# Reordering the value tiles, the weight folds and the first query logits in a fused linear-attention and dense kernel

## Chip, core and metric

The kernel runs on one core of a Trainium2 chip. The metric is the device time of one execution in microseconds (us), lower is better. Each kernel was executed several times, and the runs of the kernel before and of the kernel compared with it were taken on the same chip in the same rounds. A ratio is the mean time of one kernel's runs over the mean of the other's in the same rounds, so it isn't quite the ratio of the medians quoted beside it.

## The reference, cut to what matters

```python
# x: 2048 x 512, 32 heads of 16
qkv = x @ wqkv
pq, pk = q @ w_phi, k @ w_phi                     # per head
phi_q = concat(softmax(pq), softmax(-pq))         # the same for k
kv, z = phi_k^T v, sum(phi_k)
a = (phi_q kv) / (phi_q z + 1e-6) @ wo
b = relu(x @ w1) @ w2                             # 512 -> 1376 -> 512
g = sigmoid(sum(x * gate_w))
out = g * a + (1 - g) * b
```

## The kernel before

TensorE does nearly everything. At its start it computes the hidden layer of the first 512 rows. Then it multiplies `w_phi` into the query and key weights (eight **weight folds**, four for the query, four for the key). Then, for each of 16 tiles of 128 rows, it computes query and key **logits** (a query half and a key half of four matmuls each), the **value tile** (four matmuls), the product of key features and values (`kv`), and some **units** of the hidden layer of later rows (four matmuls each). The **gate remainder** is 16 short matmuls for 512 rows: the last 96 columns of the hidden layer, which fill no unit, and the column of the gate. The folds need the transposed weights, which arrive by DMA in two transfers, query first.

A matmul group writes to one of eight PSUM banks. VectorE (DVE) or ScalarE (ACT) copies the result out, and the next group that takes the bank waits for that copy. The helper `p.op` records an operation with the events that it waits for (`after`) and the event that it sets (`ev`). `free[bank]` is the event that frees a bank.

```python
def pre(i):                                   # a weight fold
    which, dt = i // 4, i % 4
    bank = (0, 1, 6, 7)[i % 4]
    after = [f"wqk{which}"] + [...] + free[bank]
    ...                                       # 4 matmuls into the bank
    # even i: copied by VectorE, odd i: by ScalarE
    free[bank] = [f"pc{i}"]

def atile(m):                                 # logits: query in bank 0, key in bank 1
    ...                                       # 8 matmuls, then exp(+x), exp(-x) on ScalarE
    free[1], free[0] = [emk], [f"em{m}"]

def vtile(m, eng="act", bank=2):              # a value tile, copied by `eng`
    ...

gatecol(0)
vtile(0, "dve")
vtile(1, "act", nextbank())                   # nextbank(): 3, 4, 5 in rotation
for i in range(4):
    pre(i)
vtile(2, "dve")
for i in range(4, 8):
    pre(i)
rest(0)                                       # gate remainder
...
for m in range(NT):
    atile(m)
    if m >= LAG: kv(m - LAG)
    if m + 3 < NT: vtile(m + 3)
    for u in mid[m]: unit(*u)                 # two units in the first turn
```

The softmax here doesn't subtract the row's maximum and nothing guards it: scores larger than these inputs give would overflow.

## Time and profile before

| what | value |
|---|---|
| median of the first 3 timed runs | 146.91 us (146.79 to 146.95) |
| the profiled execution itself | 147.59 us, span 146.3 us |
| TensorE busy | 98% of the span |
| folds 0 to 3 start / folds 4 to 7 start | 15.30 / 17.57 us |
| tile 1's logits start | 23.33 us |

The profile is of one execution, and that execution took 0.64 us longer than the longest of the three timed ones. The lines of this profile are in the prediction.

### The profile page before, as it was taken

Reading aid. Unit: us, or ns where it says so; the run is one execution under the profiler, and the core shown is the slowest. Engines: PE = TensorE matmul, PEld = TensorE weight load, DVE = VectorE, ACT = ScalarE, POOL = GpSimd, SP = SyncE. Lnnn points to the kernel's source line nnn. Section 1 sums busy time; section 2 is a strip of 40 time slices with the busy share of each in tenths; the row PEclk is TensorE's granted clock in tenths of the full one; section 3 lists DMA queues with packets and bytes.
Section 4 is the critical chain, followed back from the end, with each engine's and each line's share of the span. In section 5 each row is a group of like instructions: output and inputs, shape, how many; then the busy total and the mean of one; then the engine's idle time right before and its main releaser. Section 6 shows DMA issues by size and latency. Waiting matters only on the chain.

```text
span 146.3 us, 2520 instructions
## 1 busy us (share of the span) xinstructions
PE 143.0 (98%) x970; PEld 72.3 (49%) x970; DVE 91.7 (63%) x156; ACT 72.4 (49%) x124; POOL 52.2 (36%) x62
## 2 busy tenths in 40 slices
PE   8999799999999999999999999999999999999994
PEld 3444564444455545544645555554444444444443
DVE  4338627777687878678698977674445555555342
ACT  4134467798778778887878862022221111111150
POOL 2013002778768678688869820300000000000000
DMA  5998998033549984335333431354333223222213
GB/s 150 262 276 163 231 167 186 3 69 72 76 80 328 179 201 73 72 72 108 78 72 75 104 72 31 81 108 117 85 82 78 72 72 76 72 72 74 72 44 106
DMA packets 46517, 16.12 MB, mean 110 GB/s; under 512 B 40392, under 2 KB 46120, under 8 KB 46504
## 3 DMA queue, kind: packets, MB, share of 16 engines
q1 hardware_dynamic: 46352, 15.92, 50.3%
q8 instruction: 8, 0.13, 0.4%
q10 hardware_dynamic: 152, 0.03, 0.1%
q14 instruction: 5, 0.04, 0.1%
HBM read 4.15 MB, written 2.10 MB: 43 GB/s over the span
## 4 chain that ended last, share of the span: by engine, by line
PE 86%; SPq 7%; DMA 4%; DVE 1%; issue 0%
PE PS L483 26%; PE PS L328 18%; PE PS L272 18%; PE PS L492 9%; PE PS L404 8%; SPq L185 4%; DMA PHQ<-in_A_wqkv_dram 4%; PE PS L458 3%; PE PS L426 3%; PE PS L284 2%; SPq L162 2%; SPq L175 1%; PE PS L306 1%; DVE WQK L506 1%; SPq L182 0%
## 5 line engine op out<-in xcount | busy, mean ns | idle before, releaser
L483 PE MATMUL PS<-W,HT 128*128 128x512 bf16 (+4 forms) x187 | 40.6, 366 | 0.0
L372 POOL TENSOR_TENSOR EB<-EB,SC 128x1024 bf16<-128x1024 bf16 x15 | 28.9, 1930 | 23.4 <-DVE SC L370 23.4
L348 ACT ACTIVATE EB<-PS 128x480 bf16<-128x480 f32 (+1 forms) x44 | 30.1, 756 | 14.2 <-PE PS L328 14.2
L497 ACT ACTIVATE TFA<-PS,GT 128x512 bf16<-128x512 f32 x16 | 11.0, 687 | 42.7 <-PE PS L492 36.6
L272 PE MATMUL PS<-XT,W 128*128 128x512 bf16 x128 | 30.7, 379 | 0.0
L328 PE MATMUL PS<-WQK,XT 128*128 128x480 bf16 x128 | 28.5, 366 | 0.0
L368 DVE TENSOR_REDUCE ZB<-EB 128x64 f32<-128x1024 bf16 x15 | 18.3, 1220 | 14.7 <-ACT EB L348 14.7
L506 DVE SCALAR_TENSOR_TENSOR WQK<-PS,OMG,TFA 128x512 bf16<-128x512 f32 (+2 forms) x17 | 12.2, 719 | 23.6 <-ACT TFA L497 22.4
L483 PEld LDWEIGHTS PS<-W,HT 128*128 128x128 bf16 (+1 forms) x187 | 17.0, 98 | 17.4
L258 ACT ACTIVATE HT<-PS 128x512 bf16<-128x512 f32 x35 | 20.3, 614 | 7.4 <-PE PS L520 5.6
L328 PEld LDWEIGHTS PS<-WQK,XT 128*128 128x128 bf16 x128 | 12.5, 98 | 13.6
L383 DVE TENSOR_REDUCE ZB<-EB 128x64 f32<-128x1024 bf16 x16 | 18.6, 1164 | 0.0
L272 PEld LDWEIGHTS PS<-XT,W 128*128 128x128 bf16 x128 | 12.0, 98 | 13.2
L392 POOL TENSOR_TENSOR EB<-EB,SC 128x512 bf16<-128x512 bf16 x16 | 16.9, 1059 | 1.3
L404 PE MATMUL PS<-WV,XT 128*128 128x512 bf16 x64 | 16.2, 378 | 0.0
L492 PE MATMUL PS<-WO,OT 128*128 128x512 bf16 x64 | 16.1, 378 | 0.0
L468 DVE TENSOR_TENSOR WQK<-PS,RDEN 128x512 bf16<-128x512 f32 x16 | 11.1, 692 | 0.5
L492 PEld LDWEIGHTS PS<-WO,OT 128*128 128x128 bf16 x64 | 6.1, 97 | 7.2
L414 ACT ACTIVATE VS<-PS 128x512 bf16<-128x512 f32 x14 | 8.5, 608 | 2.0 <-PE PS L404 2.0
L370 DVE RECIPROCAL SC<-ZB 128x64 f32<-128x64 f32 x16 | 8.8, 553 | 0.5
L458 PEld LDWEIGHTS PS<-KVNZ,PHQ 128*128 128x128 bf16 x128 | 6.1, 97 | 3.6
L404 PEld LDWEIGHTS PS<-WV,XT 128*128 128x128 bf16 x64 | 5.4, 97 | 4.8
(57 smaller groups left out, 85.7 us busy)
## 6 DMA issues: line engine op xcount, KB each, us to landing
out_dram<-WQK SPq DMA_DIRECT2D x15, 128.0 KB, 1.7
W<-in_B_w_dram SPq DMA_DIRECT2D x2, 640.0 KB, 5.8
W<-in_B_w_dram SPq DMA_DIRECT2D x3, 256.0 KB, 3.8
WV<-in_A_wqkv_dram SPq DMA_DIRECT2D x1, 512.0 KB, 6.5
WO<-in_A_wo_dram SPq DMA_DIRECT2D x2, 256.0 KB, 3.0
W<-in_B_w_dram SPq DMA_DIRECT2D x1, 352.0 KB, 5.1
OT<-in_A_x_dram SPq DMA_DIRECT2D x2, 128.0 KB, 2.3
W<-in_B_w_dram SPq DMA_DIRECT2D x2, 128.0 KB, 3.0
```

Of the source, the lines that this page charges most:

```text
L258: p.op("act", lambda e: e.activation(dst, src, ACT.Relu), after=[f"h{c}_{kt}"], ev=ev)
L272: p.op("pe", lambda e, t=t: e.matmul(PS[:, bank, :], W1[:, t, kt * P:(kt + 1) * P], XT[:, t, c * 512:(c + 1) * 512], start=(t == 0), stop= ...
L328: p.op("pe", lambda e, dt=dt, which=which: e.matmul(PS[:, which, 0:DE], XT[:, dt, m * P:(m + 1) * P], WQK[:, which, dt * DE:(dt + 1) * DE] ...
L348: p.op("act", lambda e: e.activation(dst, s_, ACT.Exp, scale=scale), after=[f"qk{m}"] + busy, ev=ev)
L368: p.op("dve", lambda e: e.tensor_reduce(zk, ek, AX.X, ALU.add), after=[emk, f"cst{b}"], ev=f"zk{m}")
L372: p.op("pool" if m < NT - 1 else "dve", lambda e: e.tensor_tensor(EB[:, b, 3, :].rearrange("p (g f) -> p g f", f=DH), EB[:, b, 2, :].rearr ...
L383: p.op("dve", lambda e: e.tensor_reduce(ZB[:, b, 0:64].rearrange("p (h s) -> p h s", s=2), bass.AP(tensor=EB, offset=base, ap=[[EBS, P], [ ...
L392: p.op("pool", lambda e: e.tensor_tensor(EB[:, b, 0, :].rearrange("p (h s f) -> p h s f", h=H, s=2)[:, :, 1, :], EB[:, b, 1, :].rearrange( ...
L404: p.op("pe", lambda e, dt=dt: e.matmul(PS[:, bank, :], XT[:, dt, m * P:(m + 1) * P], WV[:, dt, :], start=(dt == 0), stop=(dt == NDT - 1)), ...
L483: p.op("pe", lambda e, kt=kt, M=M: e.matmul(PS[:, bank, 0:n], HT[0:M, kt, m * P:(m + 1) * P], W2[0:M, kt, cs], start=(kt == 0), stop=(kt = ...
L492: p.op("pe", lambda e, t=t: e.matmul(PS[:, bank, :], OT[:, t, m * P:(m + 1) * P], WO[:, t, :], start=(t == 0), stop=(t == NDT - 1)), after ...
L506: p.op("dve", lambda e: e.scalar_tensor_tensor(out=OSB[:, ob, cs], in0=PS[:, bank, 0:n], scalar=OMG[:, m:m + 1], in1=TFA[:, m % 2, cs], op ...
```

## The change

The intent is to give TensorE work while it waits for the two weights. Value tile 2 goes ahead of the folds. Value tile 3 and the query half of tile 0's logits go between the two groups of folds. For that the folds take other banks, and the gate remainder is the last thing ahead of tile 0's key half.

```diff
         def pre(i):
-            bank = (0, 1, 6, 7)[i % 4]
+            bank = (0, 1, 6, 7, 1, 7, 2, 6)[i]
...
-        def atile(m):
+        def atile(m, part=None):
...
-            if m == 0:
-                order = [(dt, w) for w in (0, 1) for dt in range(NDT)]
+            if part is not None:
+                order = [(dt, part) for dt in range(NDT)]
...
+            if part == 0:
+                return
...
         vtile(1, "act", nextbank())
+        vtile(2, "dve")
         for i in range(4):
             pre(i)
-        vtile(2, "dve")
+        vtile(3, "act", 6)
+        atile(0, 0)
         for i in range(4, 8):
             pre(i)
         rest(0)
...
-            atile(m)
+            atile(m, None if m else 1)
...
-            if m + 3 < NT:
+            if 0 < m < NT - 3:
                 vtile(m + 3)
```

More of the change, by code (lines that the diff above doesn't have):

```diff
@@ L332, in atile @@
                     + ([f"pc{4 * which + c}" for c in range(4)] if m == 0 and dt == 0 else []),
-                    ev=(f"qk{m}" if i == 7 else None))
+                    ev=(f"qk{m}" if part != 0 and i == len(order) - 1 else None))
+            if part == 0:
+                return
             src = PS[:, 0:2, 0:DE].rearrange("p a (h f) -> p a h f", h=H)
```

## The prediction

> **What bounds the kernel now.** I read the page first, then the chain that ended last in order of time, then the waits of TensorE, then the timeline of the 12 us in which the change works. Page and chain:
>
> ```profile
> PE 143.0 (98%) x970; PEld 72.3 (49%) x970; DVE 91.7 (63%) x156; ACT 72.4 (49%) x124; POOL 52.2 (36%) x62
> ...
> PE 86%; SPq 7%; DMA 4%; DVE 1%; issue 0%
> ...
> 12.41 5.12 DMA PHQ<-in_A_wqkv_dram
> 17.53 0.04 issue
> 17.57 1.01 PE PS L306 x16
> 18.59 0.69 PE PS L284 x16
> 19.28 1.62 PE PS L328 x8
> 20.90 0.86 PE PS L404 x4
> 21.76 1.73 PE PS L272 x8
> ```
>
> TensorE is busy 98% of the span and is 86% of the chain. Before 17.57 us the chain is a DMA, the second transposed projection weight; from 17.57 us to 143.73 us it is TensorE alone. So whatever moves TensorE's stream near 20 us moves the end by as much, and nothing later absorbs it. How much there is to win, the waits of TensorE say:
>
> ```profile
> PE PS L306 <- DMA PHQ<-in_A_wqkv_dram: 0.9, 2, 0.5
> PE PS L231 <- DVE ONE L207: 0.4, 1, 0.4
> ```
>
> Only two waits lie in the stretch of the change: the two halves of the weight folds (L306), each waiting for its weight. The timeline of that stretch:
>
> ```profile
> 13.95 0.69 DVE L412 CAST VS<-PS 128x512 bf16<-128x512 f32 x1
> ...
> 15.30 1.01 PE L306 MATMUL PS<-Wbd,PHQ 128*128 128x120 bf16 x16 [0.52 <-DMA PHQ<-in_A_wqkv_dram]
> 15.72 1.22 DVE L311 CAST WQK<-PS 128x480 bf16<-128x480 f32 x2 [1.07 <-PE PS L306]
> 15.93 1.03 ACT L313 ACTIVATE WQK<-PS 128x480 bf16<-128x480 f32 x2 [0.52 <-PE PS L306]
> ...
> 16.15 1.03 PE L404 MATMUL PS<-WV,XT 128*128 128x512 bf16 x4
> ...
> 17.57 1.01 PE L306 MATMUL PS<-Wbd,PHQ 128*128 128x120 bf16 x16 [0.40 <-DMA PHQ<-in_A_wqkv_dram]
> ...
> 19.12 1.78 PE L328 MATMUL PS<-WQK,XT 128*128 128x480 bf16 x8
> ...
> 20.94 1.83 ACT L348 ACTIVATE EB<-PS 128x960 bf16<-128x960 f32 x2 [1.06 <-PE PS L328]
> ...
> 23.33 1.78 PE L328 MATMUL PS<-WQK,XT 128*128 128x480 bf16 x8
> ```
>
> The shown ends of matmuls overlap their successors, so I count by starts. Value tiles 0 and 1 start at 12.89 and are issued by 12.89 + 2 x 0.86 = 14.61; the first fold starts at 15.30: a gap of 0.69. Value tile 2 starts at 16.15 and is issued by 17.01; the fifth fold starts at 17.57: a gap of 0.56. In all **1.25 us** (0.92 in the view, which lets the drain of the pipe count as busy). That is 0.85% of 146.91 us and the most that this change can save.
>
> **What the Trainium skill says.** (1) "TensorE: Matmul & The Clock Gate", section "Wait — 56ns, not 53.3ns?": warm back-to-back matmuls start N / 2.4 GHz + 2.5 ns apart, 215.7 ns at N = 512. The trace agrees: the chain counts four of them at 0.86 us. (2) Same page, section "What's actually happening": the clock falls back after an idle window of some 3.4 us. The gaps here stay well below, and the trace has a granted clock of 1.00 through them, so I charge no slow matmuls. (3) "PSUM — Partial Sum Buffer", section "PSUM bank collisions raise a hardware error": the hardware doesn't arbitrate two engines on one bank, so a semaphore must guard it. Hence a matmul group that takes a bank again stands behind the copy that empties it. No wait of this kind stops TensorE in the trace before. (4) Same page, section "Engine vs sequencer instructions": the queues of VectorE and ScalarE are strict FIFO. The trace agrees in that the copies of a pair come one after the other (0.652 us each, 1.22 us for two, so 0.57 from start to start). So a value copy put ahead of fold copies delays them.
>
> **The change part by part.** No operation is added or removed; order and banks change. All parts keep their durations. The new order on TensorE is value tiles 0, 1, 2; folds 0 to 3; value tile 3 into bank 6; the query half of tile 0's logits; folds 4 to 7; the gate remainder; the key half; then the loop, which no longer has value tile 3. Terms from the trace: a value tile 0.86; a half of the logits 1.62 / 2 = 0.81; a fold (15.30 to 16.15, four) 0.21; the remainder (18.42 to 19.12) 0.70. From a fold's first matmul to its copy 0.42 (15.30 to 15.72); from the start of a value tile's last matmul (13.54) to its copy 0.41. VectorE to TensorE release 0.06 (the constant's memset ends at 0.32, the first matmul starts at 0.38), used for ScalarE also, an estimate.
>
> Step 1, value tile 2 before the folds. It takes bank 2 from value tile 0, whose copy ends at 13.95 + 0.69 = 14.64. So it starts at 14.70 in place of 14.61 (gap **0.09**) and is issued by 15.56. The first weight had landed by 15.29, so the first wait is gone: folds 0 to 3 take 15.56 to 16.41.
>
> Step 2, value tile 3 in bank 6. Bank 6 holds fold 2, and fold 2 is copied by VectorE, third in a queue: first the copy of value tile 2 (ready at 14.70 + 0.65 + 0.41 = 15.76, to 16.45), then fold 0 (starts 0.61 after, the spacing of a 0.69 us operation in this trace, at 16.37), then fold 2 (0.57 later, 16.94, ends 17.60). Value tile 3 can start at 17.66, though TensorE was free at 16.41: a gap of **1.25**. This is the new wait that matters. The tile is issued by 18.52, the query half by 19.33 (its folded weights are ready).
>
> Step 3, folds 4 to 7, 19.33 to 20.18. The second weight landed by 17.57, hidden. Their banks 1, 7, 2, 6 are free (value tile 3's copy on ScalarE, 18.73 to 19.33, is done before fold 7 at 19.97). The remainder takes until 20.88. The key half needs all four copies: VectorE's second runs 20.32 to 20.97, ScalarE's second 20.42 to 20.99, so it starts at 21.05: a gap of **0.17**. Issued by 21.86.
>
> Step 4, the first tile of the loop. Before, value tile 3 and two hidden-layer units (0.86 + 1.73 = 2.59 us) lay between tile 0's logits and tile 1's, and covered the exponentials. Now only 1.73 us lie there. The exponentials start 0.40 after the last logit matmul's start (20.54 to 20.94), here 21.66 + 0.40 = 22.06, take 1.83 and end at 23.89. Tile 1, whose banks they empty, starts at 23.95; TensorE was free at 23.59: a gap of **0.36**. From then on each turn has its value tile again and more than the 2.1 us cover, and the trace shows no wait.
>
> Sum: old gaps 1.25 go, new gaps 0.09 + 1.25 + 0.17 + 0.36 = 1.87 come. Tile 1's logits start at 23.95 in place of 23.33, with the same work done: **+0.62 us**. Nothing behind absorbs it, as TensorE waits nowhere later; 146.91 + 0.62 = 147.5.
>
> **Rivals.** (a) The intent holds, the value tile and the query half fill both waits and no new one comes: -1.25, 145.7 us. For it: the order of the operations is just long enough to cover the landing of the weights at 15.3 and 17.6. Against it: bank 6, whose copy is third in VectorE's queue. (b) Only the bank-6 wait is real and the exponentials don't hold tile 1: gaps 1.51, +0.26, 147.2 us. For it: step 4 rests on an overlap of 0.36 us only. Against it: 1.83 of exponentials, 0.40 of drain and 0.06 of release are all from rows, and 2.29 minus a matmul's 0.20 exceeds 1.73. (c) The transfers are hidden, but each of four restarts of TensorE costs 0.1 us more than the one release that I could measure: +1.0, 147.9 us. For it: the release is read off one wait at the kernel's start. (d) VectorE becomes a bound for a while, because all its copies come late: against it, VectorE is 63% busy, and the first use of tile 0's key features by TensorE is at 33.5 us, when POOL has had them since 26.6.
>
> **Range and chances.** (b) and (c) lie 0.3 to 0.4 us on either side of 147.5, and runs of the kernel before spread over 0.16 us. I take 146.9 to 148.1 for eight times in ten; what is outside is mostly (a) in full or in part. Two per cent is 2.94 us: faster would need more than twice the idle time that exists, slower nearly five times my net. So within 2% at 0.98, and 0.01 for each side.
>
> **What would show it.** In the waits of TensorE the two DMA waits are gone, and in their place stand a wait of L404 for VectorE's fold copy (near 1.1 to 1.3 us, near 17.7 us in time), a small one of L328 for a fold copy near 21.0, and one of L328 for ScalarE's exponentials near 23.9. VectorE's timeline has the value copy, then two fold copies in a row, ending near 17.6. The two starts to compare: tile 1's logits, 23.33 before. If they come earlier than 23.33, steps 2 and 4 are wrong; if the wait at value tile 3 is there and the one at tile 1 isn't, (b) holds. A fold start later than 15.6, or a granted clock below 1.0 after the long gap, would be outside of all that I reckoned with.

## The result

The changed kernel took 148.66 us (median of 6 runs, 148.27 to 149.25) against 146.94 us of the kernel before (6 runs, 146.79 to 147.27), a ratio of 1.0116 with a 95% interval of 1.0089 to 1.0143. It is slower by 1.7 us where 0.6 us was predicted, and lies above the predicted range.

The page of the changed kernel's profile (its profiled run took 148.50 us, near the median) has these lines for engine shares and for the chain that ended last, which answer to the first two shown of before:

```profile
PE 142.6 (97%) x954; PEld 72.5 (49%) x970; DVE 91.7 (62%) x156; ACT 72.5 (49%) x124; POOL 52.1 (35%) x62
...
PE 95%; DVE 2%; ACT 1%; issue 1%; DVEq 0%
```

The DMA has gone from the chain. In its place VectorE and ScalarE stand in it. The chain in order of time (start, length, engine and line), in the stretch of the change:

```profile
13.21 2.72 PE PS L406 x12
15.94 0.02 issue
15.96 0.69 DVE VS L414
16.65 1.14 DVE WQK L311 x2
17.79 0.05 issue
17.84 1.04 PE PS L406 x4
...
21.22 0.10 issue
21.32 0.98 PE PS L328 x4
22.30 0.02 issue
22.32 1.84 ACT EB L350 x2
24.17 0.05 issue
24.21 0.98 PE PS L328 x4
```

Value tiles 0 to 2 run through; then the chain passes through VectorE, which copies value tile 2 and then two folds, and comes back to TensorE at 17.84 us with value tile 3. It leaves TensorE again at 22.32 us for ScalarE's exponentials and comes back with tile 1's logits at 24.21 us. The waits of TensorE say the same (who waited for whom, total, times, longest):

```profile
PE PS L406 <- DVE WQK L311: 1.1, 1, 1.1
PE PS L231 <- DVE ONE L207: 0.4, 1, 0.4
PE PS L328 <- ACT EB L350: 0.2, 1, 0.2
```

Both waits for the weights are gone, and two waits of the predicted kind are there. The two smaller ones that were predicted are in the list of the weight loader (PEld), which loads a matmul's weights ahead of it:

```profile
PEld PS L406 <- DVE VS L414: 0.4, 1, 0.4
PEld PS L328 <- DVE WQK L311: 0.2, 1, 0.2
```

The view shows TensorE's waits somewhat short, because a matmul's modelled end lies after the time at which the next one could have started (a 128x512 matmul is shown 378 ns long on average, and four follow each other in 0.86 us). From the starts in the timeline of the changed kernel

```profile
13.07 2.85 PE L406 MATMUL PS<-WV,XT 128*128 128x512 bf16 x12
...
15.76 1.00 PE L306 MATMUL PS<-Wbd,PHQ 128*128 128x120 bf16 x16
...
19.52 1.00 PE L306 MATMUL PS<-Wbd,PHQ 128*128 128x120 bf16 x16
20.36 0.86 PE L284 MATMUL PS<-W,XT 128*128 128x97 bf16 x16
```

the gaps are: 13.07 + 3 x 0.862 = 15.66 to 15.76, so 0.10 within the value tiles (value tile 2 starts at 14.89, 1.82 after value tile 0, where two tiles take 1.72); 15.76 + 0.85 = 16.61 to 17.84, so 1.23 ahead of value tile 3; 20.36 + 0.69 = 21.05 to 21.32, so 0.27 ahead of the key half; and 21.32 + 0.81 + 1.73 = 23.86 to 24.21, so 0.35 ahead of tile 1. In all 1.95 us.

So the stretch can be measured by one number: the time from the start of value tile 0 to the start of tile 1's logits. It holds the same work in all orders: four value tiles 3.45, folds 0.85 + 0.84, remainder 0.69, tile 0's logits 1.62, two units 1.73, together 9.18 us. What exceeds 9.18 is gaps. (Spans are printed to 0.1 us, so what is counted to the end is good to 0.05 us.) In the changed kernel it is 24.21 - 13.07 = 11.14 us. In the first profile of the kernel before it was 23.33 - 12.89 = 10.44 us. That explains 0.70 us of the difference, not 1.7. From tile 1's logits to the end both profiles have the same: 147.2 - 24.21 = 122.99 and 146.3 - 23.33 = 122.97 us. The missing microsecond isn't behind the change. It had to be in the profile that the change was compared with.

### The profile page after: what moved, and what is told of

The parts are those of the page before. It is cut to its first block, busy times and chain, and to the rows that moved or that the text cites. A ratio compares the mean times of both kernels' runs of the same rounds, so it can differ in the third digit from the quotient of the medians.

```text
span 147.2 us, 2503 instructions
## 1 busy us (share of the span) xinstructions
PE 142.6 (97%) x954; PEld 72.5 (49%) x970; DVE 91.7 (62%) x156; ACT 72.5 (49%) x124; POOL 52.1 (35%) x62
## 4 chain that ended last, share of the span: by engine, by line
PE 95%; DVE 2%; ACT 1%; issue 1%; DVEq 0%
PE PS L485 25%; PE PS L328 18%; PE PS L272 17%; PE PS L406 9%; PE PS L494 9%; PE PS L522 5%; PE PS L460 3%; PE PS L428 3%; PE PS L284 2%; PE PS L231 2%; ACT EB L350 1%; DVE WQK L311 1%; DVE WQK L508 1%; PE PS L237 1%; PE PS L306 1%
## 5 line engine op out<-in xcount | busy, mean ns | idle before, releaser
L485 PE MATMUL PS<-W,HT 128*128 128x512 bf16 (+4 forms) x183 | 40.1, 366 | 0.2
L272 PE MATMUL PS<-XT,W 128*128 128x512 bf16 x122 | 29.9, 379 | 0.3
L406 PE MATMUL PS<-WV,XT 128*128 128x512 bf16 x60 | 15.3, 379 | 1.3 <-DVE WQK L311 1.1
```

The source lines that it names most:

```text
L272: p.op("pe", lambda e, t=t: e.matmul(PS[:, bank, :], W1[:, t, kt * P:(kt + 1) * P], XT[:, t, c * 512:(c + 1) * 512], start=(t == 0), stop= ...
L406: p.op("pe", lambda e, dt=dt: e.matmul(PS[:, bank, :], XT[:, dt, m * P:(m + 1) * P], WV[:, dt, :], start=(dt == 0), stop=(dt == NDT - 1)), ...
L485: p.op("pe", lambda e, kt=kt, M=M: e.matmul(PS[:, bank, 0:n], HT[0:M, kt, m * P:(m + 1) * P], W2[0:M, kt, cs], start=(kt == 0), stop=(kt = ...
```

## The experiments

Theory A: the predicted waits are right, but the profile of the kernel before is of an execution in which the second weight landed late, so that the gaps that the change removes are in most runs much smaller than 1.25 us. Rival B: the profile is typical, and the changed kernel loses a further microsecond that its own profile doesn't show. Fourteen runs were made, two of them of the unchanged kernels, with 5 rounds each and 6 executions of the kernel (4 in pad_after, 5 in late_w_after). All gave correct results. They ran in four batches on different chips, so a ratio is always to the kernel before in the same batch. Starts and stretches are those of one profiled execution each.

| run | median us | ratio to before (95% interval) | value tile 0 starts | tile 1's logits start | between | to the end |
|---|---|---|---|---|---|---|
| before, first profile | 146.94 | 1 | 12.89 | 23.33 | 10.44 | 122.97 |
| r_before | 146.68 | 0.9988 (0.9970 to 1.0005) | 12.89 | 22.33 | 9.44 | 122.97 |
| pad_before | 147.05 | 1.0006 (0.9980 to 1.0032) | 13.05 | 22.22 | 9.17 | 122.98 |
| late_w_before | 147.18 | 1.0026 (1.0008 to 1.0044) | 13.50 | 22.67 | 9.17 | 123.03 |
| later_w_before | 148.28 | 1.0087 (1.0069 to 1.0105) | 13.78 | 24.08 | 10.30 | 123.02 |
| after, first profile | 148.66 | 1.0116 (1.0089 to 1.0143) | 13.07 | 24.21 | 11.14 | 122.99 |
| r_after | 148.61 | 1.0115 (1.0093 to 1.0138) | 13.68 | 24.82 | 11.14 | 122.98 |
| pad_after | 148.88 | 1.0133 (1.0115 to 1.0151) | 13.08 | 24.22 | 11.14 | 122.98 |
| late_w_after | 148.38 | 1.0109 (1.0089 to 1.0129) | 12.98 | 24.11 | 11.13 | 122.99 |
| later_w_after | 148.67 | 1.0117 (1.0097 to 1.0137) | 13.26 | 24.39 | 11.13 | 123.01 |
| free_bank | 148.49 | 1.0100 (1.0070 to 1.0131) | 13.56 | 23.84 | 10.28 | 123.66 |
| late_copy | 148.06 | 1.0084 (1.0046 to 1.0121) | 13.01 | 22.99 | 9.98 | 123.71 |
| all_three | 148.25 | 1.0074 (1.0041 to 1.0107) | 13.37 | 23.86 | 10.49 | 123.14 |
| between | 147.51 | 1.0026 (0.9995 to 1.0057) | 13.25 | 22.67 | 9.42 | 123.63 |
| late_copy5 | 147.22 | 1.0031 (1.0007 to 1.0054) | 13.43 | 23.41 | 9.98 | 122.99 |
| between5 | 146.55 | 0.9985 (0.9964 to 1.0005) | 13.46 | 22.82 | 9.36 | 122.98 |

### Both kernels profiled again

The kernel before, unchanged:

> The kernel before, unchanged, profiled a second time. The first profiled run took 147.59 us against a median of 146.94, so its profile may show a late arrival of the second folded weight. Theory A (my gaps of 1.25 us were those of an unusually slow run): the new profile has a span near 145.6 to 145.9 us and the fifth fold starts at 16.8 to 17.2 us in place of 17.57, so that the two gaps ahead of the folds come to about 0.6 to 0.9 us. Rival B (the profile was typical and the profiled execution is just longer): the fifth fold again at 17.5 to 17.6 us, span 146.3. Ratio 1.00 either way.

The timeline of this second profile of the kernel before, TensorE's rows:

```profile
12.89 1.89 PE L404 MATMUL PS<-WV,XT 128*128 128x512 bf16 x8
14.61 1.00 PE L306 MATMUL PS<-Wbd,PHQ 128*128 128x120 bf16 x16
15.45 1.03 PE L404 MATMUL PS<-WV,XT 128*128 128x512 bf16 x4
16.58 1.01 PE L306 MATMUL PS<-Wbd,PHQ 128*128 128x120 bf16 x16
...
22.33 1.78 PE L328 MATMUL PS<-WQK,XT 128*128 128x480 bf16 x8
```

Value tile 0 starts at the same 12.89 us. But the first fold follows the value tiles at once (14.61), and the fifth starts at 16.58 us in place of 17.57: the gaps are 0 and 16.58 - (15.45 + 0.86) = 0.27 us, not 0.69 and 0.56. Tile 1's logits start 1.00 us earlier than in the first profile, and the span is 145.3 us in place of 146.3. TensorE's list of waits has no DMA any more. Only the weight loader, whose idle time isn't covered by modelled ends, still shows one:

```profile
PEld PS L306 <- DMA PHQ<-in_A_wqkv_dram: 0.6, 1, 0.6
```

The profiled execution took 146.62 us this time. The first took 147.59, which is above all eleven runs of the kernel before in these rounds (146.68 to 147.31). Theory A holds in kind: the first profile was of a slow execution. Its numbers were missed on the far side (gaps of 0.6 to 0.9 us, a fifth fold at 16.8 to 17.2 and a span from 145.6 us were expected), and this second execution is a fast one, below all eleven of the kernel before. With its stretch the kernels should differ by 11.14 - 9.44 = 1.70 us; 0.0115 of 147 us is 1.69. That a single fast profile fits so well is in part luck: the gap also depends on when value tile 0 starts, and what it is in the median execution wasn't measured.

Where the late weight comes from can be followed one step back. SyncE (SPq) issues the two weight transfers, here in the first and then in the second profile:

```profile
6.60 8.06 SPq L185 DMA_TRANSPOSE PHQ<-in_A_wqkv_dram  x2
6.59 7.31 SPq L185 DMA_TRANSPOSE PHQ<-in_A_wqkv_dram  x2
```

In the chain of the first profile the second weight's transfer starts at 12.41 us and lands at 17.53; in that of the second it is

```profile
11.54 4.99 DMA PHQ<-in_A_wqkv_dram
```

so it lands at 16.53. Of the 1.00 us, 0.87 was lost before the transfer began. In the twelve profiles in which nothing was put between the two transfers, their issue takes 8.06 us in the first profile and 6.92 to 7.67 in the other eleven: the first profile is the odd one out. Why its issue took longer isn't known.

The changed kernel, unchanged:

> The changed kernel, unchanged, profiled a second time. Ratio 1.010 to 1.013 again. The chain of the first profile starts on TensorE at 0.38 us and never passes through a weight's arrival, so theory A expects the span to differ from 147.2 us by just as much as the start of value tile 0 differs from 13.07 us (within 0.1 us), and the distance from there to tile 1's logits to be 11.14 us again. Rival: the distance itself varies by several tenths.

Value tile 0 started 0.61 us later (13.68 for 13.07), tile 1's logits 0.61 later (24.82), and the span is 147.8 for 147.2 us. The 11.14 us between are the same to the hundredth; the other profiles of this order have 11.13 or 11.14. The waits that the change made don't vary in these profiles; the waits that it removed do.

### A delay at TensorE's start

```diff
         gatecol(0)
+        pad(2)            # two 128x512 matmuls of ones into bank 7, unused
         vtile(0, "dve")
```

> Kernel before with two more 128x512 warm-up matmuls (0.43 us of TensorE at full clock) put right ahead of value tile 0, outputs unused. Theory (before, the wait for the second weight absorbs what delays TensorE's first 13 us): under 0.1 us longer, ratio 1.000 to 1.001. Rival (TensorE's start is on the path in this kernel too): +0.43 us, ratio 1.003.

> The same two matmuls in the changed kernel. Theory (with the weights hidden, nothing absorbs a delay at the start): +0.43 us on the changed kernel of the same rounds, so ratio to before about 0.003 more than that run's. Rival (there is slack in the changed kernel as well): no longer than the changed kernel.

The times don't decide: both kernels grew by 0.0018 over the unchanged ones of the same rounds, and the intervals overlap. The start of value tile 0 varies by itself between 12.6 and 13.8 us (12.62 is where it would have been in the padded kernel before without the padding), more than the 0.43 us added. In the one profile of the padded kernel before there is no gap at all left ahead of the folds (9.17 us in the table), so there the delay took the place of a wait. That before absorbs such delays in general is argued, not shown.

### The second weight made late

```diff
         for i in range(2):
+            if i:                       # load of wo moved here from the loop
+                p.dma("sp", ... WO[:, 0:2, :] ...)      # late_w: half of it
             p.dma("sp", ... transposed query / key weight i ...)
```

> Kernel before with half of the output projection's weight (256 KB, needed only after 94 us) loaded ahead of the second folded weight instead of in the loop, so that the second folded weight lands some 0.7 to 1.5 us later (an estimate from 0.66 us of issue and 3.0 us to landing for such a load). Theory (this kernel's time follows the landing of that weight, and the first profile was one of a late landing): the fifth fold starts 0.7 to 1.5 us later than 16.58, and everything behind it shifts by as much, ratio 1.005 to 1.010. Rival (landing is hidden in an ordinary run): ratio 1.000.

> The same move in the changed kernel, whose fifth fold starts at 19.5 us. Theory (the change hides the landing with some 2 us to spare): no change, ratio 1.010 to 1.013 as without it, and 11.14 us from value tile 0 to tile 1's logits. Rival (the transfers matter to it too, or the first x block comes too late): ratio above 1.015.

The kernel before became 0.0026 slower, less than expected, and its profile shows no wait: it fell on one of the two fastest executions of its six (146.96 us), and value tile 0 started late there (13.50 us). The load had slid into time in which the DMA queue stood anyway. The changed kernel kept its 1.0109 and 11.13 us, as expected. The delay was too small to settle it, so the whole of `wo` was moved.

> Kernel before with the whole output projection's weight (512 KB) loaded ahead of the second folded weight. Half of it had cost 0.0026, and in its profile the next transfer was issued at 13.94 us, just as without it: the load had slid into time in which the queue stood anyway. Theory (this kernel waits for that weight whenever it lands late): the weight lands another 1 us or so later, the fifth fold waits again as in the first profile, at 17.3 us or later, with a DMA wait of TensorE in the list; ratio 1.005 to 1.012. Rival (a landing up to 1 us later is still hidden): ratio 1.003 or less, no such wait.

> The same in the changed kernel. Theory (its fifth fold is held back to 19.5 us by VectorE's queue, not by the weight): ratio 1.010 to 1.013, 11.14 us from value tile 0 to tile 1's logits, no DMA wait. Rival: ratio above 1.015.

The kernel before with the late weight has the wait of the first profile again, first in the list of TensorE's waits, then in the timeline:

```profile
PE PS L311 <- DMA PHQ<-in_A_wqkv_dram: 1.0, 1, 1.0
```

```profile
18.32 1.01 PE L311 MATMUL PS<-Wbd,PHQ 128*128 128x120 bf16 x16 [0.96 <-DMA PHQ<-in_A_wqkv_dram]
```

It is 0.0087 slower, as expected. The changed kernel with the same late weight has a ratio of 1.0117, as without it, and its longest wait is still that for the fold copy, with no DMA among them:

```profile
PE PS L411 <- DVE WQK L316: 1.1, 1, 1.1
```

So the landing of the second weight sets the time of the kernel before when it is late, and the changed kernel doesn't feel it. Its intent worked. Only the second weight was delayed here; the 0.69 us of the first profile ahead of fold 0 were a wait for the first. With the weight this late the two differ by only 0.4 us (148.28 and 148.67; their stretches differ by 0.83, but value tile 0 started 0.52 us later in this profile of the kernel before).

### The new waits taken away one by one

Value tile 3 in a free bank:

```diff
-        vtile(3, "act", 6)
+        vtile(3, "act", nextbank())
```

> The changed kernel with value tile 3 in the next bank of the hidden layer's rotation (bank 3, emptied long before) in place of bank 6. Theory (the bank is what holds TensorE): the wait of the value tile for a fold copy goes; value tile 3 follows fold 3 at once, 1.23 us earlier counted from value tile 0. The query half then waits for fold 2's copy, so the net is 0.87 us: from value tile 0 to tile 1's logits 10.27 us in place of 11.14, time near 147.75 us, ratio near 1.0055. Rival (the gap is a queue or issue effect of the new order, not the bank): value tile 3 starts as late as before, ratio 1.011.

The stretch shrank from 11.14 to 10.28 us, as expected to a hundredth. Value tile 3 now starts at 17.08, right behind folds that start at 16.24. The bank was what held TensorE. But the time fell only to a ratio of 1.0100, because the rest of the kernel grew from 122.98 to 123.66 us (see below).

Value tile 2 copied behind the folds, in addition:

```diff
-        vtile(2, "dve")
+        vtile(2, "dve", copy=False)
         for i in range(4):
             pre(i)
+        vcopy(2, "dve", 2)
```

> As the free-bank run, and VectorE copies folds 0 and 2 ahead of value tile 2. Theory (the value copy at the head of VectorE's queue delays the fold copies by 0.39 us): the query half starts right behind value tile 3, from value tile 0 to tile 1's logits 9.9 us, time near 147.4 us, ratio near 1.003. Rival (ScalarE's copies are the later ones): no gain over the free-bank run.

The stretch is 9.98 us (9.9 expected): the place in VectorE's queue costs 0.30 us on top of the bank. The time again fell short, for the same reason as in the run before. The list of waits of this run names it:

```profile
PE PS L490 <- ACT HT L258: 0.5, 1, 0.5
```

Line 490 is the first output projection of the dense branch, at 88 us. It takes bank 4. `nextbank()` had been called once more than in the kernel before, so the rotation of banks 3, 4, 5 stood one further through the whole loop, and the last hidden-layer unit fell on bank 4. The projection had to wait for its ReLU. This was a fault of the experiment, in four runs.

The exponentials covered, in addition:

```diff
-    VB = 6
+    VB = 7
...
-            if 0 < m < NT - 3:
-                vtile(m + 3)
+            if m < NT - 4:
+                vtile(m + 4)
```

> As the late-copy run, and the loop's value tiles run one ahead (value tile 4 in the first turn, seven value buffers), so that the exponentials of tile 0 are covered by 2.59 us of TensorE work again. Theory: tile 1's logits wait for ScalarE no more, another 0.35 us: from value tile 0 to tile 1's logits, less the value tile's own 0.86, 9.55 us; time near 147.05 us, ratio near 1.0007. Rival (the short wait of tile 1 is made up later): no gain over the late-copy run, ratio 1.003.

The stretch, less the value tile's 0.86, is 9.63 us (9.55 expected), and tile 1's wait is gone. But the time isn't lower than that of the late-copy run beyond the noise. The bank fault is in it too, and with all value tiles one turn ahead, turn 12 has none: there tile 13's weight load waits 0.6 us for the exponentials. The wait was moved, not removed.

The late-copy kernel again, without the fault:

```diff
-        vtile(3, "act", nextbank())
+        vtile(3, "act", 5)
```

> The late-copy run again, with value tile 3 in bank 5 by name, so that the rotation of banks 3, 4, 5 in the hidden layer isn't shifted. In the free-bank, late-copy, all-three and in-between runs the shift made the first output projection at 88 us wait 0.5 us for the last ReLU on bank 4. Theory: that wait is gone, 9.98 us from value tile 0 to tile 1's logits as before, 122.97 us from there to the end of the span; time near 147.4 us, ratio near 1.003. Rival (the loss behind tile 1 has another cause): ratio 1.008 again.

Stretch 9.98 us, 122.99 us from there to the end, ratio 1.0031, all as expected. Giving value tile 3 a free bank and the fold copies precedence takes back 0.0085 of the 0.0116 (two ratios of different batches). What is left over 9.18 us is 0.10 ahead of value tile 2, 0.10 ahead of the query half, 0.26 ahead of the key half and 0.36 ahead of tile 1.

### A version built from the reading

```diff
 # on the kernel before; bank = (0, 1, 6, 7, 1, 7, 6, 2)[i]
         vtile(2, "dve")
+        atile(0, 0)                       # query half: 0.81 us more of cover for the weight
         for i in range(4, 8):
             pre(i)
-        rest(0)
+        vtile(3, "act", nextbank())       # covers the last fold copies
 ...
+            if m == 0: rest(0)            # with two units it covers the exponentials
```

> A version built from the reading: kernel before, with the query half put between value tile 2 and fold 4 (0.81 us more to cover the second weight), value tile 3 between fold 7 and the key half (it covers the last fold copies), and the gate remainder behind the key half in the first turn, so that 0.70 + 1.73 us cover the exponentials. Theory: no wait on TensorE from value tile 0 on; tile 1's logits 9.2 us after value tile 0 (the same work without a gap) in place of 9.44, time near 146.6 us, ratio 0.997 to 0.999. Rival (a new wait, for the first x block's transfer or for ScalarE, which now does the remainder behind the exponentials): ratio 1.000 or above.

The stretch was 9.42 us, no better than the kernel before in its second profile (the copy of value tile 1 on ScalarE held the query half by 0.17 us), and the bank fault cost 0.65 us behind it. Without the fault, and with that copy behind ScalarE's fold copies:

> The in-between version with value tile 3 in bank 5, and ScalarE's copy of value tile 1 behind its fold copies (they had held the query half by 0.17 us). Theory: 9.25 us from value tile 0 to tile 1's logits, 122.97 us from there to the end; 0.2 us less than the kernel before in a run with an early weight and up to 1 us less in one with a late weight; ratio 0.997 to 0.999. Rival (TensorE's later start in some runs, now unabsorbed, takes it back): ratio 1.000.

The stretch is 9.36 us (9.25 expected), 122.98 us from there to the end, ratio 0.9985 with an interval of 0.9964 to 1.0005. Its list of TensorE's waits has nothing left but the one at the kernel's very start:

```profile
PE PS L231 <- DVE ONE L207: 0.4, 1, 0.4
```

From the starts, 0.09 us are left ahead of each half of tile 0's logits. By its order it should hide 0.81 us more of a late weight than the kernel before; it was not run with one. That it is faster is likely but not clear of the noise. No version clearly faster than the kernel before was found.

## Why the prediction was wrong

**What bounds the kernel** was right: TensorE's stream sets the end, and nothing behind tile 1 absorbs a delay. From tile 1's logits to the end it is 122.97 to 123.03 us in all ten profiles of the two orders; the padding and the moved loads change none of TensorE's work behind that point.

**Steps 1 to 4, the new waits,** were right in place and nearly in size. The prediction had 0.09 + 1.25 + 0.17 + 0.36 = 1.87 us; the profile has 0.10 + 1.23 + 0.27 + 0.35 = 1.95. The step that was least exact is the key half (0.17 against 0.27): ScalarE's last fold copy ended at 21.17 us and the key half started at 21.32, 0.15 later, where 0.06 had been assumed for such a release. That the long one is the wait of bank 6 behind VectorE's queue was confirmed by taking both away: 0.86 us came back with the bank, another 0.30 with the queue's order. One of the prediction's signs of being wrong seems to have come, a fold start later than 15.6 us (15.76). But value tile 0 started 0.18 us later than in the profile before, and so the fold is where it was expected.

**The step that failed** is the first term of the sum, "old gaps 1.25 go". It was read correctly from the profile, but the profile was of an execution with a late weight. In the second profile of the kernel before the gaps were 0 and 0.27 us. With this size the prediction's own sum is 1.87 - 0.27 = +1.60, or 148.5 us, near what was measured; with both terms as measured, 1.95 - 0.27 = 1.68 against 1.7 us. The mechanism was right, and the mis-sized term is the gain. That 0.27 stands for ordinary executions rests on the fit of the times and on three profiles with 0.27, 0 and 0; its mean wasn't measured.

The warning was on hand. The profiled execution had taken 147.59 us, the timed ones 146.79 to 146.95. An excess of 0.7 us in a kernel whose TensorE stream is fixed from 20 us on most likely lies ahead of 20 us, and there the prediction had just read 1.25 us of waits on transfers. Adding the +0.62 to the median, as the prediction did, mixed the gaps of a slow execution with the time of ordinary ones. Had it been added to 147.59, it would have given 148.2.

**The rivals.** (a), the intent without new waits, failed by bank 6. (b), no wait at tile 1, failed: the wait is there with 0.35 us. (c), slower restarts of TensorE, failed for three of the four restarts and holds for one: after VectorE's copies ended at 14.83 and 17.79 us TensorE started at 14.89 and 17.84, and after ScalarE's exponentials at 24.17 it started at 24.21, so these cost 0.04 to 0.06 us where 0.06 was assumed. The one ahead of the key half cost 0.15, and that is nearly the whole miss of that step. That no matmul ran slow after the long gap, which the prediction took for granted, is shown by the four of value tile 3: they take 0.87 us (17.84 to 18.71). (d), VectorE as a bound for longer, isn't seen: the distance from tile 1's logits to the end didn't change. None of the rivals was the one that mattered, that the profile itself might be an outlier.

**The range and chances.** The range allowed for errors in the new waits and none for the size of the old ones. The class, within 2%, was right.

## What to carry to other kernels

Before you count what a change can save, compare the profiled execution's own time with the timed runs; where it is longer, the waits that vary from run to run (here those for transfers) may be too big in it, and a second profile of the same kernel costs little. Work that is moved to cover one wait is taken from somewhere: here value tile 2 had covered the fold copies and value tile 3 the exponentials, and both waits came into the open. When a group of matmuls is given another bank, look at who empties that bank and how much stands ahead of it in that engine's queue, and don't shift a rotation of banks that something much later relies on.

## What the Trainium skill lacked or had wrong

- "Perfetto Trace Analysis", section "Optimization Strategy", says to find the gaps on the busiest engine and what blocks it. It doesn't say that one trace may hold gaps that most executions lack: 1.25 us of waits for the weights in one profile of the kernel before, 0.27 us in the next, none in those of two padded or delayed variants.
- "TensorE: Matmul & The Clock Gate", section "What's actually happening", has the warm-up of the clock, says that it varies by run, and puts it under 1% of a typical span. Traces agree: the weight loads of the first hidden-layer matmuls start 0.43 us apart, twice the later 0.22, until 4.4 us in pad_after and until 6.3 us in r_after, and value tile 0 starts at 12.65 (the padding taken off) and 13.68 us. What the page lacks is that this is as large as the effects that one wants to measure in a tuned kernel (1.0 us between these two, against a change of 1.7). Over all profiles the start varies by 1.2 us; that all of this is the warm-up isn't shown, since waits for transfers lie in the same stretch (0.27 us at 5.03 us in the first profile).
- "TensorE: Matmul & The Clock Gate", section "Seeing it yourself", warns that the clock events of a trace can be unreliable. Neither it nor another page has that the mean granted clock of a profile may not show the warm-up. The following rows are from the view of stretches, from 4 to 6.3 us. The first is of the changed kernel's second profile:

```profile
4.00:6.30 2.30, 2.30 (x6) 0.73 (x5) 0.56 (x5) 0.31 (x1) 0.00 (x0) 1.00 1.11 283
```

The second is of its padded variant:

```profile
4.00:6.30 2.30, 2.30 (x11) 1.03 (x10) 0.56 (x3) 0.13 (x1) 0.00 (x0) 1.00 1.09 272
```

The first count is TensorE's matmuls, 6 and 11: nearly twice as many in the same time. The third number from the end is the granted clock, 1.00 in both. So the 1.00 doesn't rule out a slow start.
